# A spectral filter beside a feed-forward product: two kinds of step change places in each slot, and one small copy changes its engine

## The chip, the cores and the metric

The kernel runs on one core of one Trainium2 chip. The core has TensorE (PE, matrix products into PSUM), VectorE (DVE), ScalarE (ACT), GpSimd (POOL) and SyncE (SP); SP, ACT and POOL also issue DMAs. Each engine works through its own list of instructions in order and waits on semaphores for the others. The metric is the time of one execution on the device, in microseconds (us).

## The reference

The input `x` has 2048 rows and 1024 columns. The layer norm of it goes two ways: through a filter in the frequency domain, and through a feed-forward product with a hidden width of 3584.

```
xn  = layernorm(x)
s   = irfft2(rfft2(xn) * (w_r + 1j * w_i), (2048, 1024))
h   = silu(xn @ w1)            # 2048 x 3584
out = x + s * silu(h @ w2)     # 2048 x 1024
```

## The kernel before

TensorE works in float16 and gets near float32 by splitting each operand into a high and a low half and adding three products: high by high, high by low, low by high. A split has two instructions: `high` on ScalarE (L257, the value rounded to f16) and `low` on VectorE (L260, the rest).

The feed-forward product comes in two parts. The **first product** fills the first 635 us: w1 by the rows of `xn`, in 112 pieces `pa` of 24 matmuls. The hidden values are combined and written to device memory as the left sides of a Strassen-like scheme with seven products. The **second product** fills the rest: for each of the seven products `m` (0 to 6) and each of eight row blocks `j` there is a PSUM tile `pb{m}_{j}`, made of two half-products (`k` = 0, 1) of 21 matmuls of 128x512 (L549 to L551). Each half-product needs its hidden values, `ht{m}_{j}_{k}`, loaded by a DMA that ACT issues (L525), and its half of w2, `w2_{m}_{k}`. Finished tiles are added by VectorE and ScalarE into `kept` and `pl` tiles, stored, and at the end combined with the filter's result (`fs`, `fx`) into the output.

w2 is made ready while the second product runs. There are 98 blocks `jr0` to `jr97`, 14 to each product. A step of `w2_gen` loads the block four ahead by a DMA on SP (L420), for products 4 and 5 adds a second block into the one three ahead by an accumulating DMA on POOL (L424; it waits for the first load to land), and then issues the high of its own block and the low of the block before it.

The filter has a forward transform, the multiplication by w, edge terms (`edge`, whose result comes back through memory as the tile `zps`) and an inverse transform. The inverse treats four groups of columns `c` in the order `IORDER = (1, 3, 0, 2)`. For each, `load_i` (L1234) loads its spectrum into the one tile `zt{c}` and the constants `kk{c}`, `edge_in` (L1246) copies the edge column into the tile, and `i_gen` (L1255) then makes, in steps: four matmul groups `iu{c}_{g}` (L1281 or L1289) in two PSUM buffers; for each, a copy `uc` of half of it by ScalarE (L1295), sum and difference `ub` by VectorE (L1297, L1298), which free the PSUM buffer, a butterfly (`up`, `uu`) on VectorE, and a split into `us` (L1360, L1361); then, when all four `us` are there, four matmul groups `id{c}_{p}` (L1371), which read the constants `cis`, with butterflies `sk`, `spa` and `s` on VectorE. The name `tag="ft"` is that of the two PSUM buffers that `iu` and `id` share.

The order of all instructions is set while the program is built, by Python generators. After each half-product of the second product the program calls `work()`, one **slot**. A slot gives one step to the queue `wq` (w2's steps), one to `xq`, and up to three to `bg` (transform, filter, inverse), until a step answers `PAUSE` or until the planner's own clock of VectorE is past its clock of TensorE by more than `LEAD`, 1.0 us. So what stands first in a slot stands first on every engine and in every DMA queue that its step uses. `while ready2[0] < ...` ahead of a half-product draws further w2 steps if the half of w2 that it needs isn't made yet.

The DMAs that SP and ACT issue share eight semaphores in turn; a DMA is issued when the one before it on its semaphore has landed.

Of the kernel before, what the change touches and what calls it, by code (L numbers as in the profile page):

```python
# [26 lines left out]
IORDER = (1, 3, 0, 2)  # L27
# [105 lines left out]
def spectral_ffn(ctx, tc, x, w_r, w_i, w1, w2, ca, kc, ci, tw, pm, out):  # L133
    nc = tc.nc
# [35 lines left out]
    zps = cp.tile([128, 2, 4, 4, 2], F16, name="zps")  # L170
# [284 lines left out]
    done2, ready2, chunks = [0], [-1], [0]  # L455
# [790 lines left out]
    def edge_in(c):  # L1246
        zt = C["z"][c]
        if c % 2:
            zt = zt.rearrange("m (e q h l i) -> m e q h l i", e=2, q=4, h=2, l=8)
            nc.gpsimd.tensor_copy(zt[:, :, :, :, 0, 0], zps[:, :, c])  # L1250
        else:
            zt = zt.rearrange("m (q h r l i) -> m q h r l i", q=4, h=2, r=2, l=8)
            nc.gpsimd.tensor_copy(zt[:, :, :, :, 0, 0], zp[:, c].rearrange("m r q h -> m q h r"))

    def i_gen(c):  # L1255
        ip = C["p"]
        tt, stt = nc.vector.tensor_tensor, nc.vector.scalar_tensor_tensor
        if c == IORDER[0]:
            edge_in(c)
# [187 lines left out]
        for p in range(5):  # L1447
            if p < 4:
                mat2(p)
            if p:  # L1450
                bfly(p - 1)
            if p == 3 and c != IORDER[-1]:
                edge_in(IORDER[IORDER.index(c) + 1])
            yield 3.4 if p else 0.3
# [13 lines left out]
    def slot(q):  # L1468
        while q:
            job = q[0]  # L1470
            cost = job.step()
            if not job.done:
                return cost
            if q and q[0] is job:
                q.pop(0)
        return 0
# [19 lines left out]
    with tc.manual_schedule():  # L1496
        bg, wq, xq = [], [], []
# [20 lines left out]
        def after(ev):  # L1518
            settle()
            fresh_ev[0] = ev  # L1520
            tick()
            work()

        def work():
            slot(wq)
            count[0] += 1
            if count[0] % 8:
                slot(xq)
            clock["dve"] = max(clock["dve"], clock["pe"] - 1.0)
            for _ in range(3):  # L1530
                if clock["dve"] > clock["pe"] + LEAD or hold[0] or slot(bg) == PAUSE:
                    break

        nc.gpsimd.memset(ones, 1.0)
        idle = ones.bitcast(F16)
# [105 lines left out]
        for n, (m, j) in enumerate(seq):  # L1641
# [14 lines left out]
            for k in range(2):  # L1656
                while ready2[0] < m * NP + 7 * k + 6:
                    slot(wq)
                mm2(m, j, ps, k)
                if k == 0:  # L1660
                    settle()
                    load_parts(m, j)
                    ahead_rows(m, j)
                    if (m, j) == (6, 6):
                        load_parts(m, 7)
                        ahead_rows(m, 7)
                    tick()
                    work()
# [43 lines left out]
```

## Time and profile before

| | us |
|---|---|
| three runs | 1228.38, 1229.09, 1229.4 |
| profiled execution: time | 1229.27 |
| profiled execution: span | 1227.5 |
| TensorE busy | 1211.4 (99%) |
| VectorE busy | 1003.7 (82%) |
| ScalarE busy | 496.1 (40%) |
| GpSimd busy | 140.2 (11%) |

The span goes from the first to the last instruction; the profiled execution's time is 1.8 us more. The granted TensorE clock is 1.000 over the span. Numbers of the profile are on the span's own clock. A row of a chain or a timeline begins with the start and the length in microseconds; a bracket at its end gives the engine's idle time ahead of it and what ended that. The profile leaves out the numbers in tile names: `zt` there is `zt1` or another, `jr` any block of w2; which one a row is follows from its place in the program's order.

### The profile page before, as it was taken

What the parts mean: (1) busy time and instruction counts of PE and PEld (TensorE: products, weight loads), DVE (VectorE), ACT (ScalarE), POOL (GpSimd) and SP (SyncE); (2) the same over time, 40 slices, a digit from 0 to 9 for tenths busy, and PEclk for the clock granted to TensorE, in tenths of its full rate; (3) what the DMA queues carried; (4) which work ended last, traced back from release to release, by engine and by line L of the source; (5) the groups of instructions that cost most, each with busy time, mean ns of one, the idle gap of its engine ahead of it and who ended that gap; (6) DMA issues with size and microseconds to landing.
All of it is one profiled execution on the core that took longest, in us unless ns stands there. A gap on an engine that the chain in (4) does not pass through costs nothing.

```text
span 1227.5 us, 19143 instructions
## 1 busy us (share of the span) xinstructions
PE 1211.4 (99%) x6992; PEld 615.1 (50%) x6992; DVE 1003.7 (82%) x2006; ACT 496.1 (40%) x670; POOL 140.2 (11%) x256
## 2 busy tenths in 40 slices
PE   8999999999999999999999999999999999999998
PEld 5544445445444544445445555554445554455545
DVE  7778997898798798958969989995377876997766
ACT  6775553455375654434423222221122322333212
POOL 3320100002010000201101121152111111000000
PEclk9999999999999999999999999999999999999999
DMA  8887585747678978489998999977979999996677
GB/s 251 184 195 188 165 255 180 211 130 214 192 254 276 317 231 270 146 259 208 188 282 279 263 253 233 315 255 221 269 218 302 264 338 310 305 364 244 224 249 274
DMA packets 285055, 299.98 MB, mean 244 GB/s; under 512 B 48928, under 2 KB 211744, under 8 KB 284576
## 3 DMA queue, kind: packets, MB, share of 16 engines
q1 hardware_dynamic: 264944, 239.95, 66.9%
q10 hardware_dynamic: 15840, 50.67, 11.8%
q0 software_dynamic: 4176, 8.13, 3.6%
q8 instruction: 55, 0.90, 0.3%
q14 instruction: 40, 0.33, 0.1%
HBM read 188.05 MB, written 104.35 MB: 238 GB/s over the span
## 4 chain that ended last, share of the span: by engine, by line
PE 59%; DMA 15%; DVE 14%; ACT 3%; issue 3%; SPq 1%; POOL 1%; ACTq 0%; DVEq 0%; POOLq 0%
PE pa L466 33%; PE pb L551 7%; PE pb L549 7%; PE pb L550 7%; DMA jr<-in_B_w_dram 2%; PE id L1371 2%; DMA jr<-ws 1%; DVE Z L1124 1%; DVE w L260 1%; DMA cis<-in_ci_dram 1%; DMA ht<-hd_dif 1%; ACT xp L750 1%; DMA vq<-vd 1%; DMA zd<-zq 1%; DMA zt<-zd 1%
## 5 line engine op out<-in xcount | busy, mean ns | idle before, releaser
L466 PE MATMUL pa<-xnT,w 128*128 128x512 f16 x2688 | 584.3, 379 | 1.3 <-ACT w L257 0.7
L466 PEld LDWEIGHTS <-w 128*128 128x128 f16 x2688 | 261.2, 98 | 312.7 <-issue 1.2
L549 PE MATMUL pb<-w,ht 128*128 128x512 f16 (+2 forms) x812 | 300.4, 372 | 0.0
L550 PE MATMUL pb<-w,ht 128*128 128x512 f16 (+2 forms) x812 | 300.4, 372 | 0.0
L551 PE MATMUL pb<-w,ht 128*128 128x512 f16 (+2 forms) x812 | 300.3, 372 | 0.0
L551 PEld LDWEIGHTS <-ht 128*128 128x128 f16 x812 | 79.4, 98 | 91.1
L549 PEld LDWEIGHTS <-ht 128*128 128x128 f16 x812 | 79.5, 98 | 86.7
L550 PEld LDWEIGHTS <-ht 128*128 128x128 f16 x812 | 79.4, 98 | 86.8
L475 ACT ACTIVATE h<-pa,s 128x512 f32<-128x512 f32 x112 | 75.6, 677 | 77.6 <-PE pa L466 60.2
L257 ACT ACTIVATE w<-jr,sc 128x512 f16<-128x512 f32 x98 | 68.4, 713 | 86.4 <-DMA jr<-in_B_w_dram 45.6
L260 DVE SCALAR_TENSOR_TENSOR w<-jr,sc,w 128x512 f16<-128x512 f32 x98 | 71.3, 743 | 18.8 <-ACT w L257 18.8
L257 ACT ACTIVATE hosum<-hr,hs 128x1536 f16<-128x1536 f32 x28 | 44.0, 1573 | 87.5 <-DVE hr L505 34.9
L260 DVE SCALAR_TENSOR_TENSOR hoone<-h,hs,hoone 128x2048 f16<-128x2048 f32 x28 | 65.6, 2342 | 7.2 <-ACT hoone L257 7.2
L257 ACT ACTIVATE hoone<-h,hs 128x2048 f16<-128x2048 f32 x28 | 55.9, 1995 | 28.6 <-issue 11.1
L504 DVE TENSOR_TENSOR hr<-h 128x1024 f32<-128x1024 f32 x28 | 34.1, 1219 | 21.8 <-ACT h L475 21.8
L260 DVE SCALAR_TENSOR_TENSOR hosum<-hr,hs,hosum 128x1536 f16<-128x1536 f32 x28 | 50.7, 1810 | 1.4 <-ACT hosum L257 1.4
L257 ACT ACTIVATE w<-w1r,rs 128x1024 f16<-128x1024 f32 x28 | 31.9, 1143 | 37.7 <-DVE w L260 24.2
L642 ACT ACTIVATE pl<-pl,c 128x512 f32<-128x512 f32 (+2 forms) x28 | 17.7, 656 | 70.2 <-DVE pl L618 43.6
L424 POOL DMA_DIRECT2D jr<-in_B_w_dram x28 | 24.6, 999 | 180.3 <-DMA jr<-in_B_w_dram 89.7
L1124 POOL TENSOR_TENSOR Z<-yb 128x32 f32<-128x32 f32 x32 | 16.2, 525 | 209.0 <-DVE yb L1103 202.2
L1033 ACT ACTIVATE zq<-Z,zs 128x1024 f16<-128x1024 f32 x16 | 18.4, 1148 | 52.5 <-DVE Z L1124 25.6
L260 DVE SCALAR_TENSOR_TENSOR w<-w1r,rs,w 128x1024 f16<-128x1024 f32 x28 | 35.6, 1273 | 2.3 <-ACT w L257 2.2
(239 smaller groups left out, 1571.6 us busy)
## 6 DMA issues: line engine op xcount, KB each, us to landing
w1r<-in_B_w_dram SPq DMA_DIRECT2D x28, 512.0 KB, 6.6
hd_sum<-hosum SPq DMA_DIRECT2D x56, 256.0 KB, 2.9
hd_one<-hoone SPq DMA_DIRECT2D x56, 256.0 KB, 4.0
hd_dif<-hoone SPq DMA_DIRECT2D x56, 256.0 KB, 4.3
w2m<-in_B_w_dram SPq DMA_DIRECT2D x28, 512.0 KB, 5.6
ht<-hd_dif ACTq DMA_DIRECT2D x32, 448.0 KB, 9.2
jr<-in_B_w_dram SPq DMA_DIRECT2D x56, 256.0 KB, 6.7
ht<-hd_sum ACTq DMA_DIRECT2D x32, 448.0 KB, 5.7
```

Source lines behind the costliest of these rows:

```text
L257: nc.scalar.activation(hi, raw, AF.Copy, scale=scale)
L260: nc.vector.scalar_tensor_tensor(lo, raw, scale, hi, op0=OP.mult, op1=OP.subtract)
L424: nc.gpsimd.dma_start(raw[n], w2_block(*todo[n], 1), accum_op=OP.add)
L466: nc.tensor.matmul(ps, w[:, wh, d], xt[:, xh, d], start=(n == 0), stop=(n == 23))
L475: nc.scalar.activation(hq[:, 2 * (c % 2) + f % 2], ps, AF.Silu, scale=s1[:, f:f + 1])
L504: tt(sums[:, 0:2], hq[:, 0::2], hq[:, 1::2], op=OP.subtract)
L549: nc.tensor.matmul(ps, hh[:, 0], w[:, 0], start=first, stop=False)
L550: nc.tensor.matmul(ps, hh[:, 0], w[:, 1], start=False, stop=False)
L551: nc.tensor.matmul(ps, hh[:, 1], w[:, 0], start=False, stop=last)
L1033: nc.scalar.activation(zqs[q][:, 0, :, 16 * j:16 * j + 16], zs_[u], AF.Copy, scale=zs)
L1124: eng.tensor_tensor(Z[:, ns, pos], x0[:, :, ls], x1[:, :, ls], op=o_)
L1371: nc.tensor.matmul(ps[:, g, cols], us[g][:, uh, 4 * r + p], C["ci"][:, ch, g, r, cols], start=(r == 0 and n == 0), stop=(r == 1 and n == 2 ...
```

## The change

In the second product (`chunks[0] == 4`) a slot's step of w2 comes after the steps of `bg`. In the first product it stays ahead. And the copy of the edge column for the first group of the inverse, `c = 1`, is made by VectorE; those of the other three groups stay on GpSimd. The computation is the same, and so are the instructions but for that one.

```diff
@@ edge_in
         if c % 2:
             zt = zt.rearrange("m (e q h l i) -> m e q h l i", e=2, q=4, h=2, l=8)
-            nc.gpsimd.tensor_copy(zt[:, :, :, :, 0, 0], zps[:, :, c])
+            (nc.vector if c == IORDER[0] else nc.gpsimd).tensor_copy(zt[:, :, :, :, 0, 0], zps[:, :, c])
@@ work
         def work():
-            slot(wq)
+            if chunks[0] < 4:
+                slot(wq)
             count[0] += 1
             if count[0] % 8:
                 slot(xq)
             clock["dve"] = max(clock["dve"], clock["pe"] - 1.0)
             for _ in range(3):
                 if clock["dve"] > clock["pe"] + LEAD or hold[0] or slot(bg) == PAUSE:
                     break
+            if chunks[0] == 4:
+                slot(wq)
```

In the lists below, a row is the line, the kind of instruction, the tile written and the tiles read; the last number in a name counts buffers.

SP's list where the inverse is opened, in the last slots of product 2; before:

```order
L420 DMA jr53_8542<-in_B_w2_dram 128x512
L1215 DMA zps_220<-zpd_87 64x4x8 x4
L420 DMA jr54_8572<-in_B_w2_dram 128x512
L1239 DMA zt1_8581<-zd1_84 64x8x512 x4
L1243 DMA kk1_8586<-in_kc_dram 128x2064
L1229 DMA cis_8580<-in_ci_dram 128x4096
L420 DMA jr55_8619<-in_B_w2_dram 128x512
```

The same place after:

```order
L420 DMA jr53_8542<-in_B_w2_dram 128x512
L1215 DMA zps_220<-zpd_87 64x4x8 x4
L1239 DMA zt1_8577<-zd1_84 64x8x512 x4
L1243 DMA kk1_8582<-in_kc_dram 128x2064
L1229 DMA cis_8576<-in_ci_dram 128x4096
L420 DMA jr54_8588<-in_B_w2_dram 128x512
L420 DMA jr55_8619<-in_B_w2_dram 128x512
```

The load of `jr54` has moved behind `zt1`, `kk1` and `cis`. On POOL the copy into `zt1` stood there, before:

```order
L424 DMA jr56_8644<-in_B_w2_dram 128x512
L424 DMA jr57_8675<-in_B_w2_dram 128x512
L424 DMA jr58_8701<-in_B_w2_dram 128x512
L1250 COPY zt1_8581<-zps_220 128x16
L424 DMA jr59_8733<-in_B_w2_dram 128x512
```

It now stands on DVE, between the lows of `jr54` and `jr55`, after:

```order
L598 TENSOR_TENSOR kept5_7103<-kept5_7103,pb2_5_8652 128x512
L260 SCALAR_TENSOR_TENSOR w2_3_1_8544<-jr54_8588,sc2_234,w2_3_1_8544 128x512
L1250 COPY zt1_8577<-zps_220 128x16
L260 SCALAR_TENSOR_TENSOR w2_3_1_8544<-jr55_8619,sc2_234,w2_3_1_8544 128x512
L598 TENSOR_TENSOR kept6_7180<-kept6_7180,pb2_6_8710 128x512
```

In this place DVE otherwise has the same rows as before, and ACT has the high of `jr54`, the loads of `ht3_0_0` and `ht3_0_1`, and the high of `jr55` in this order in both programs.

ACT's list in product 4, where group `c = 0` of the inverse begins (`uc0_0` is the copy that starts to empty the PSUM of `iu0_0`); before:

```order
L525 DMA ht4_7_0_10426<-hd_one_3_1_97 128x1792
L525 DMA ht4_7_1_10428<-hd_one_3_1_97 128x1792
L257 ACTIVATE w2_5_1_10302<-jr81_10299,sc2_234 128x512
L1295 ACTIVATE uc0_0_10520<-iu0_0_10470 128x512
L1341 ACTIVATE up0_0_10526<-ub0_0_10522 128x8
L1342 ACTIVATE up0_0_10526<-ub0_0_10522 128x8
L642 ACTIVATE pl4_4_1_10383<-pl4_4_1_10383,c2_233 128x512
L257 ACTIVATE w2_5_1_10302<-jr82_10327,sc2_234 128x512
L1360 ACTIVATE us0_0_10588<-uu0_0_10525 128x1024
```

The same place after:

```order
L525 DMA ht4_7_0_10426<-hd_one_3_1_97 128x1792
L525 DMA ht4_7_1_10428<-hd_one_3_1_97 128x1792
L1295 ACTIVATE uc0_0_10516<-iu0_0_10466 128x512
L1341 ACTIVATE up0_0_10522<-ub0_0_10518 128x8
L1342 ACTIVATE up0_0_10522<-ub0_0_10518 128x8
L257 ACTIVATE w2_5_1_10302<-jr81_10299,sc2_234 128x512
L642 ACTIVATE pl4_4_1_10383<-pl4_4_1_10383,c2_233 128x512
L1360 ACTIVATE us0_0_10584<-uu0_0_10521 128x1024
L1295 ACTIVATE uc0_1_10587<-iu0_1_10491 128x512
```

`uc0_0` and the two small copies of `up0_0` have moved ahead of the high of `jr81`, and the high of `jr82` has left the rows shown: it now stands behind the two small copies of `up0_1`.

TensorE's list where the first half of `pb3_0` ends; before:

```order
L550 LDWEIGHTS ht3_0_0_8706
L550 MATMUL pb3_0_8938<-w2_3_0_8188,ht3_0_0_8706 128x512
L551 LDWEIGHTS ht3_0_0_8706
L551 MATMUL pb3_0_8938<-w2_3_0_8188,ht3_0_0_8706 128x512
L549 LDWEIGHTS ht3_0_1_8708
L549 MATMUL pb3_0_8938<-w2_3_1_8544,ht3_0_1_8708 128x512
```

The same place after:

```order
L550 LDWEIGHTS ht3_0_0_8706
L550 MATMUL pb3_0_8938<-w2_3_0_8203,ht3_0_0_8706 128x512
L551 LDWEIGHTS ht3_0_0_8706
L551 MATMUL pb3_0_8938<-w2_3_0_8203,ht3_0_0_8706 128x512
L1281 LDWEIGHTS zt1_8577
L1281 MATMUL iu1_3_8961<-kk1_8582,zt1_8577 128x128
```

The group `iu1_3` now follows the first half of `pb3_0` and not the second. In the same way `id1_0` to `id1_3` come one half-product earlier, and `iu3_0` to `iu3_3` and `id3_0` to `id3_2` one or two. From `id3_3` on TensorE's order is the same as before. In product 3, `zt3` and `kk3` are likewise loaded ahead of `jr66`, and the copy into `zt3` stands on POOL ahead of the accumulating DMA of `jr67`.

## The prediction

> **What bounds the kernel now.** I read the page's shares first, then TensorE's waits, then the stretches of time around the two long ones, then the chain that leads into each, and last what the engines in that chain had been waiting for.
>
> ```profile
> PE 1211.4 (99%) x6992; PEld 615.1 (50%) x6992; DVE 1003.7 (82%) x2006; ACT 496.1 (40%) x670; POOL 140.2 (11%) x256
> PE iu L1281 <- POOL zt L1250: 2.6, 1, 2.6
> PE iu L1289 <- DVE ub L1298: 1.8, 1, 1.8
> 860.00:880.00 20.00, 17.39 (x85) 7.80 (x83) 2.70 (x4) 0.72 (x1) 3.33 (x6) 1.00 1.02 302
> 880.00:1020.00 140.00, 140.00 (x927) 75.64 (x924) 109.75 (x285) 40.82 (x75) 19.17 (x24) 1.00 0.96 278
> 1020.00:1040.00 20.00, 18.18 (x136) 10.19 (x134) 10.77 (x21) 3.73 (x8) 1.80 (x3) 1.00 0.95 312
> 1040.00:1220.00 180.00, 180.00 (x1113) 94.97 (x1110) 142.89 (x299) 51.04 (x96) 1.13 (x2) 1.00 0.81 285
> ```
>
> TensorE is the bound. In the stretches (start and end, length, then busy time of PE, PEld, DVE, ACT, POOL; granted clock, DMA share, GB/s) it is busy without a gap from 880 to 1020 and from 1040 to 1220, short of 2.61 us before 880 and of 1.82 us before 1040, which are the two waits above. VectorE is 78% busy (109.75 of 140), so it has room. The granted clock is 1.00 in each stretch. A change that only reorders this work can win those two holes and no more; it loses wherever it makes a new one.
>
> The chain into the first hole, then what TensorE, ACT, DVE, POOL and SP show there:
>
> ```profile
> 860.43 14.25 DMA cis<-in_ci_dram
> 874.75 2.60 DMA jr<-in_B_w_dram
> 877.35 0.61 POOL jr L424 x2
> 876.73 0.38 PE L551 MATMUL pb<-w,ht 128*128 128x512 f16 x1
> 879.72 0.95 PE L1281 MATMUL iu<-kk,zt 128*128 128x128 f16 x14 [2.61 <-POOL zt L1250]
> 854.48 4.86 ACTq L525 DMA_DIRECT2D ht<-hd_sum  x2
> 875.37 0.72 ACT L257 ACTIVATE w<-jr,sc 128x512 f16<-128x512 f32 x1 [21.93 <-DMA jr<-in_B_w_dram]
> 876.12 0.75 DVE L260 SCALAR_TENSOR_TENSOR w<-jr,sc,w 128x512 f16<-128x512 f32 x1 [11.22 <-ACT w L257]
> 878.41 1.26 POOL L1250 COPY zt<-zps 128x16 f16<-128x16 f16 x1
> 865.04 12.20 SPq L420 DMA_DIRECT2D jr<-in_B_w_dram  x7
> L1239 SPq DMA_DIRECT2D zt<-zd x4: 573/783/3536, 849.2 to 851.5; - x4
> DMA to landing us min/median/max: 11.2/16.4/19.6
> ```
>
> The last two rows are those of the four `zt1` loads, issued from 849.2 to 851.5, so the copy's data was there by 851.5 + 19.6 = 871.1. But the copy stands on POOL behind three accumulating DMAs of w2, and those wait for direct loads that SP issued behind `zt1`, `kk1` and `cis`. It ran at 878.4. Matmuls start every 0.22 us here, so from the start at 876.73 to the one at 879.72 PE lost 2.99 - 0.22 = 2.8 us.
>
> The chain into the second hole:
>
> ```profile
> 1026.42 9.80 DMA jr<-in_B_w_dram
> 1036.25 0.72 ACT L257 ACTIVATE w<-jr,sc 128x512 f16<-128x512 f32 x1 [11.88 <-DMA jr<-in_B_w_dram]
> 1036.87 0.59 ACT uc L1295
> 1029.57 2.91 PE L1289 MATMUL iu<-kk,zt 128*128 128x129 f16 x48
> 1036.64 0.38 PE L551 MATMUL pb<-w,ht 128*128 128x512 f16 x1
> 1038.83 0.34 PE L1289 MATMUL iu<-kk,zt 128*128 128x129 f16 x3 [1.81 <-DVE ub L1298]
> ```
>
> `iu0_0` and `iu0_1` were through by 1032.5, but ScalarE's copy `uc0_0`, which begins to empty their PSUM, stands on ACT behind the w2 step of `jr81`, and that waited 11.9 us for an accumulating DMA. So `ub0_0` came late and `iu0_2` with it: 1038.83 - 1036.64 - 0.22 = 2.0 us.
>
> **The change part by part.** *The copy on VectorE, and SP's order.* `zt1`, `kk1` and `cis` are now issued ahead of `jr54`'s load; the copy leaves POOL's queue and stands on DVE between the lows (L260) of `jr54` and `jr55`. Its new wait is therefore `jr54`: load, high on ACT, low, copy. The trace has no such copy on VectorE; the nearest row is
>
> ```profile
> L1209 DVE SCALAR_TENSOR_TENSOR zp<-edge,zs,zp x1: 251/251/251, 836.8 to 836.8; 128x32 f16<-128x32 f32 x1
> ```
>
> so 0.25 us (tiny f16 result, like the copy), against 1.26 us as on POOL. At the late end `jr54` lands where `jr55` did, the next load behind `cis`: high from 875.37, low from 876.12 to 876.87, copy to 877.1 (at POOL's price 878.1). TensorE comes to `iu1_0` at 876.73 + 0.22 = 876.95, so the hole is 0.2 us at most (1.2 at POOL's price) instead of 2.8. At the early end the two `ht3_0` loads, which ACT issued at 854 to 859 between these transfers, now stand behind `jr54`'s high and no longer share the DMA engines. From 849.2 to 874.7 SP's loads of `zt1` (128 x 8192 f16, 2 MB), `kk1` and `cis` moved, with the page's sizes
>
> ```profile
> kk<-in_kc_dram SPq DMA_DIRECT2D x1, 516.0 KB, 17.0
> cis<-in_ci_dram SPq DMA_DIRECT2D x1, 1024.0 KB, 14.2
> ht<-hd_sum ACTq DMA_DIRECT2D x4, 448.0 KB, 7.2
> ```
>
> 3.6 MB, and `ht3_0` 0.9 MB beside them: 4.5 MB or more in 25.5 us, 0.18 MB/us. Without the 0.9 MB `cis` lands up to 5 us earlier, and the copy ends at 872 to 874, with 3 us or more to spare. I take the middle, the hole gone: -2.8 us; ends -1.6 and -2.8. The Trainium skill ("DMA: Bandwidth & Descriptors", section "Issuing engines are not separate DMA queues") says that DMAs of the scalar and sync engines run on the same 16 engines and interleave. By that rule the early end holds; if the two queues had engines of their own, the late one would, 0.2 us worse. The DMA share of 1.02 in 860 to 880, with both queues at work, agrees with it.
>
> *What pays for it there.* `ht3_0` is issued at 872 to 876 instead of 854. `pb3_0` needs it after the second `iu` pair, `pb2_7_1` and `iu1_2`.
>
> ```profile
> 882.58 0.22 PE pb L549
> 887.11 1.34 PE iu L1281 x24
> DMA to landing us min/median/max: 4.3/8.1/9.8
> ```
>
> A half-product is 887.11 - 882.58 = 4.53, so the need is at 876.95 + 2 x 1.34 + 4.53 + 1.34 = 885.5. With the longest landing of the `ht` loads in this stretch, 9.8 us, one issued at 875.5 is there at 885.3; with the median 8.1, at 883.6. Cost 0, at worst about 1.
>
> *Reordered slots.* In product 3 `iu1_3`, `id1` and `iu3_0` to `iu3_3` come one or two half-products (4.5 us each) earlier on TensorE, because VectorE's clock in the planner is no longer past its limit when their step is asked. In-order TensorE would wait if their inputs do not come forward equally.
>
> ```profile
> 889.66 0.68 DVE L1298 TENSOR_TENSOR ub<-iu,uc 128x512 f32<-128x512 f32 x1
> 897.51 1.34 PE iu L1281 x24
> 911.51 1.22 DVE L1361 SCALAR_TENSOR_TENSOR us<-uu,us 128x1024 f16<-128x1024 f32 x1
> 921.51 3.05 PE id L1371 x48
> ```
>
> Taking 2.8 us and one half-product off: `iu1_3` is reached at 897.5 - 2.8 - 4.5 = 890.2, its PSUM is freed by `ub1_1` at 890.3 - 2.8 = 887.5: 2.7 us to spare. `id1_0` is reached at 921.5 - 7.3 = 914.2, `us1_3` ends at 912.7 - 2.8 = 909.9: 4.3 to spare. Cost 0, hidden by those margins; if VectorE came later than that, each us would be a us.
>
> *w2's steps go behind.* The same 98 highs and lows, each later by at most the steps of one slot. The least margin of a low before its first matmul is in product 5:
>
> ```profile
> 1050.76 1.41 DVE L260 SCALAR_TENSOR_TENSOR w<-jr,sc,w 128x512 f16<-128x512 f32 x2
> 1067.49 0.38 PE L549 MATMUL pb<-w,ht 128*128 128x512 f16 x1
> ```
>
> The second of these lows (`jr83`'s) ends at 1052.1; by the program's order its half is begun at 1067.5, 15 us on. A slot's inverse step is 2 to 6 us of VectorE. Cost 0.
>
> *`uc0_0` ahead of `jr81`.* ACT now does `uc0_0` when `iu0_0` is done (1029.57 + 1.4, less 2.8), 8 us or more before its old place; `iu0_2` no longer waits: -2.0 us. What is late next is the low of `us0_3`, which the last quarter of `id0_0` reads:
>
> ```profile
> 1071.55 1.22 DVE L1361 SCALAR_TENSOR_TENSOR us<-uu,us 128x1024 f16<-128x1024 f32 x1 [0.43 <-ACT us L1360]
> 1073.32 2.87 PE L1371 MATMUL id<-cis,us 128*128 128x130 f16 x42
> ```
>
> It ended at 1072.8, and with half of the 3.05 us of a pair of `id` groups (the fence before last) the quarter began at 1073.5 + 3/4 x 1.53 = 1074.6: 1.8 us to spare. TensorE now comes 4.8 us sooner, so `us0_3` has to be 3.0 us sooner. Its row of VectorE work starts 8 us sooner, but w2's lows in it still wait for their accumulating DMAs. If those land 2.8 us sooner with everything else, `us0_3` is 0.2 us late at most; if not at all, up to 1.5; both are estimates, added up from the durations of that row's steps. I take 0.2.
>
> *Sum*: -2.8 - 2.0 + 0.2 = -4.6 us against the profiled execution's own 1229.27 us (span 1227.5): 1224.7. The median of the runs, 1229.09, is 0.2 below that execution, so the time is 1224.5.
>
> **The rivals.** *One hole stays or comes back.* The copy is held by `jr54`, or `us0_3` is late by 1.5 and `ht3_0` by 1. For it: the copy still waits for a transfer behind `cis`. Against: 3 us of margin if the queues share. If only the second hole goes, 1229.1 - 2.0 = 1227.1; only the first, 1226.3.
>
> *The holes only move.* The same deliveries set the pace, and the inverse's steps stall further on: 1228.5 to 1229.5. For it: DMA shares of 0.91 to 1.02. Against: both holes come from waiting in a queue behind work that was not theirs, not from a late input.
>
> *Slower: `jr54` lands late.* The copy now has w2's delivery in front of it, and both `ht3_0` loads stand behind the same high. Every us that `jr54` lands after 875.2 is one of TensorE at `iu1_0` (0.72 + 0.75 + 0.25 from landing to copy's end, need at 876.95). To end 2.5 us above the time before, the new hole has to be 2.8 + 2.0 + 2.5 = 7.3 us, with `jr54` at 882.5: 1231.6. `ht3_0`, issued at 883 and there by 893 at the longest, adds nothing, since its need moves to 892.8 with the hole. For it: this stretch has transfers of up to 19.6 us. Against: fewer bytes are in front of `jr54` than were in front of `jr55`, which landed at 875.4.
>
> *The reordering does nothing* is excluded by the order of the queues.
>
> **How the numbers follow.** Both holes gone with up to 1 us given back: 0.64, 1223.6 to 1225.8. One of them: 0.17, 1226.0 to 1227.6. Only moved: 0.08. Slower: 0.11. The range 1223.6 to 1228.2 leaves out the last two. About 0.2%, 2.5 us, is what a measurement can tell from no change. Below 1226.6 lie the first case and a third of the second: faster 0.70; same 0.18; slower 0.12.
>
> **What would show it.** Right: no TensorE wait over 0.5 us on `zt` (L1250) or `ub` (L1298); the copy, as a DVE row of 0.2 to 0.3 us, ends between 872 and 877; `uc0_0` starts within 1 us of `iu0_0`'s end; TensorE busy 20.00 of 20 us in both stretches. Wrong: a TensorE wait on `ht` at `pb3_0`, on `us` at `id0_0`, or on `zt` with the copy behind a low that waits for a `jr`.

## The result

Over 22 executions each the median went from 1229.59 us to 1226.45 us. The ratio is 0.9974, with a 95% interval from 0.9964 to 0.9984: 2.0 to 4.4 us less. In two later sets, on two chips, the changed kernel's ratio was 0.9990 (0.9975 to 1.0006) and 0.9989 (0.9972 to 1.0005). So it is faster by 3.2 us in the first set and by 1.2 and 1.4 us in the two others, whose intervals just take in no change; by none of the three ratios is it the 4.6 us that the sum gave.

Single executions scatter over all sets between about 1224 and 1234 us (changed) and 1226 and 1237 us (before). Much of that goes with the mean granted clock, which is on record for each execution. Of the 46 executions of the changed kernel in its three sets, nine have a clock of 1.000 and take 1223.84 to 1226.55 us, and the 22 at 0.997 or below take 1227.91 to 1234.37 us. Of the 82 executions of the kernel before in the three sets that followed the first, twelve have 1.000 and take 1226.17 to 1229.29 us. The means of these two groups with the full clock, 1225.2 and 1228.0, differ by 2.8 us.

Both holes are gone. These are, of the changed kernel, the page's shares, the one row in TensorE's list of waits that lies behind 640 us, and the stretches that answer to those shown of before:

```profile
PE 1213.9 (99%) x6992; PEld 616.3 (50%) x6992; DVE 1004.1 (82%) x2007; ACT 494.7 (40%) x670; POOL 137.0 (11%) x255
PE eps L1161 <- POOL edge L1154: 1.1, 1, 1.1
860.00:880.00 20.00, 20.00 (x94) 9.06 (x93) 3.21 (x6) 1.44 (x2) 3.63 (x4) 1.00 1.05 316
880.00:1020.00 140.00, 140.00 (x928) 75.78 (x927) 111.83 (x291) 39.84 (x74) 18.67 (x23) 1.00 0.95 277
1020.00:1040.00 20.00, 20.00 (x147) 11.30 (x146) 10.89 (x21) 5.65 (x10) 1.75 (x2) 1.00 1.02 305
```

TensorE is busy 20.00 of 20 us in both stretches that had a hole. The engines at the first place, in the timeline of the changed kernel, and the copy `uc0_0` at the second:

```profile
873.77 0.72 ACT L257 ACTIVATE w<-jr,sc 128x512 f16<-128x512 f32 x1 [19.01 <-DMA jr<-in_B_w_dram]
874.53 0.75 DVE L260 SCALAR_TENSOR_TENSOR w<-jr,sc,w 128x512 f16<-128x512 f32 x1 [6.57 <-ACT w L257]
875.20 0.20 DVE L1250 COPY zt<-zps 128x16 f16<-128x16 f16 x1
880.66 2.84 PE L1281 MATMUL iu<-kk,zt 128*128 128x128 f16 x48
1032.13 0.60 ACT L1295 ACTIVATE uc<-iu 128x512 f32<-128x512 f32 x1 [4.08 <-DMA ht<-hd_one]
```

The copy waits for `jr54`, as it was read from the order; it takes 0.20 us on VectorE and is done at 875.40, with TensorE there at 880.66. `uc0_0` starts at 1032.13, about 0.2 us behind the matmuls of `iu0_0`, and no longer waits for the DMA of `jr81`.

TensorE came late to both places, though, and the reason is the one wait in the list that the kernel before does not have. It stands at the nine small matmuls of the edge step (`eps`, L1161 to L1163), between `pb1_7` and `pb2_0`. First the kernel before, then the changed one. Of the timeline: TensorE's last matmul of `pb1_7` and first edge matmul, GpSimd's first edge copy, and VectorE's row that leads there; and the stretch from 808 to 812, whose third number from the end is the granted clock.

```profile
804.63 0.38 PE L551 MATMUL pb<-w,ht 128*128 128x512 f16 x1
804.84 0.30 PE L1161 MATMUL eps<-edge,perm 128*128 128x24 f32 x2
804.18 0.37 POOL L1154 COPY edge<-xsv 128x24 f32<-128x24 f32 x1
796.61 1.28 DVE L1038 SCALAR_TENSOR_TENSOR zq<-Z,zs,zq 128x1024 f16<-128x1024 f32 x1 [2.45 <-ACT zq L1033]
798.94 1.22 DVE L1086 TENSOR_TENSOR T<-X,wq 128x1024 f32<-128x1024 f32 x1
800.19 0.69 DVE L1099 TENSOR_TENSOR T<-T,T 128x512 f32<-128x512 f32 x1
808.00:812.00 4.00, 4.00 (x27) 2.08 (x26) 4.00 (x8) 0.37 (x2) 0.00 (x0) 1.00 0.98 328
```

```profile
805.21 0.38 PE L551 MATMUL pb<-w,ht 128*128 128x512 f16 x1
806.66 0.40 PE L1161 MATMUL eps<-edge,perm 128*128 128x24 f32 x2 [1.07 <-POOL edge L1154]
806.24 0.37 POOL L1154 COPY edge<-xsv 128x24 f32<-128x24 f32 x1
798.14 1.29 DVE L1038 SCALAR_TENSOR_TENSOR zq<-Z,zs,zq 128x1024 f16<-128x1024 f32 x1 [4.22 <-ACT zq L1033]
800.48 1.22 DVE L1086 TENSOR_TENSOR T<-X,wq 128x1024 f32<-128x1024 f32 x1
801.62 0.74 DVE L260 SCALAR_TENSOR_TENSOR w<-jr,sc,w 128x512 f16<-128x512 f32 x1
802.28 0.68 DVE L1099 TENSOR_TENSOR T<-T,T 128x512 f32<-128x512 f32 x1
808.00:812.00 4.00, 4.00 (x18) 2.10 (x18) 3.90 (x10) 1.52 (x3) 0.48 (x4) 0.61 1.02 214
809.47 0.63 PE L550 MATMUL pb<-w,ht 128*128 128x512 f16 x1
809.90 0.63 PE L551 MATMUL pb<-w,ht 128*128 128x512 f16 x1
```

Two things are to be seen. A low of w2 (`jr41`'s, L260 at 801.62) now stands in the middle of the filter's steps, and from the low of `zq` to the edge copy it takes 806.24 - 798.14 = 8.10 us instead of 7.57. Beside that, ScalarE's `zq` ahead of it came later. And after the wait of 1.2 us the granted clock is 0.61 in the next 4 us: 512-column matmuls start every 0.43 us instead of 0.22. The trace's record of the clock has it at half for 3.41 us, from 808.90 on. TensorE loses the wait of 1.2 us, some 1.7 us to the clock, and 0.2 us at the edge matmuls themselves, which take longer here.

The whole second product can be put in one table. All 6992 matmuls stand in each trace (7004 in `fill` below, which has twelve more), so the time between the first matmuls of named half-products can be taken from their starts. The stretches are: *edge*, from the start of `pb1_7`'s second half to the start of `pb2_1`; *zt1*, from there to `pb4_0`; *uc0*, from there to `pb5_0`; *rest*, to the last matmul. From `pb0_0` to the edge stretch it is 165.18 us in every execution. The first line is the kernel before in us; the others are differences to it.

| kernel | edge | zt1 | uc0 | rest |
|---|---|---|---|---|
| before | 17.71 | 155.59 | 86.11 | 162.85 |
| changed | +3.14 | -2.79 | -1.99 | 0.00 |
| changed, second and third execution (runs below) | +3.83, +6.01 | -2.79, -2.79 | -1.99, -1.99 | 0.00, 0.00 |
| before, second execution (run below) | +0.54 | +1.58 | -0.30 | 0.00 |

The two gains are the predicted 2.8 and 2.0 us, and the same in each of the three executions of the changed kernel. What was not in the sum is the first column.

### The profile page after: what moved, and what is told of

Its sections match the earlier page's. It is cut to its first block, busy times and chain, and to the rows that moved or that the text cites. A ratio compares the mean times of both kernels' runs of the same rounds, so it can differ in the third digit from the quotient of the medians.

```text
span 1226.4 us, 19138 instructions
## 1 busy us (share of the span) xinstructions
PE 1213.9 (99%) x6992; PEld 616.3 (50%) x6992; DVE 1004.1 (82%) x2007; ACT 494.7 (40%) x670; POOL 137.0 (11%) x255
## 4 chain that ended last, share of the span: by engine, by line
PE 69%; DMA 10%; DVE 10%; ACT 3%; issue 2%; SPq 1%; POOL 0%; ACTq 0%; DVEq 0%; POOLq 0%
PE pa L466 33%; PE pb L549 10%; PE pb L550 10%; PE pb L551 10%; DMA zd<-zq 2%; PE id L1371 2%; DMA ht<-hd_dif 2%; DMA wq<-in_A_w_i_dram 1%; ACT xp L750 1%; DMA jr<-ws 1%; DMA jr<-in_B_w_dram 1%; PE iu L1289 1%; DMA ws<-wd 1%; PE iu L1281 1%; DVE wd L383 1%
## 5 line engine op out<-in xcount | busy, mean ns | idle before, releaser
L260 DVE SCALAR_TENSOR_TENSOR w<-jr,sc,w 128x512 f16<-128x512 f32 x98 | 71.9, 744 | 17.9 <-ACT w L257 17.8
L260 DVE SCALAR_TENSOR_TENSOR hoone<-h,hs,hoone 128x2048 f16<-128x2048 f32 x28 | 65.6, 2342 | 6.9 <-ACT hoone L257 6.9
L260 DVE SCALAR_TENSOR_TENSOR hosum<-hr,hs,hosum 128x1536 f16<-128x1536 f32 x28 | 50.7, 1811 | 1.4 <-ACT hosum L257 1.4
L260 DVE SCALAR_TENSOR_TENSOR w<-w1r,rs,w 128x1024 f16<-128x1024 f32 x28 | 35.6, 1273 | 2.3 <-ACT w L257 2.2
```

The costliest lines, as they stand in the source:

```text
L260: nc.vector.scalar_tensor_tensor(lo, raw, scale, hi, op0=OP.mult, op1=OP.subtract)
```

## The experiments

Theory: each hole is a fixed arrival less TensorE's own time; the change takes two arrivals out of w2's queue, and makes a third one, the edge copies, later. Rivals: the edge wait is an accident; or deliveries set the pace, so that a hole closed at one place opens at the next.

**The changed kernel again** (`after_again`, no edit).

> The changed kernel once more. My theory, three holes that add up: both old holes of TensorE are gone (no wait on zt before iu1_0, none on ub before iu0_2), and a new one stands at the edge matmuls (L1161 to L1163) near 806 us, because GpSimd's edge copies now come after one more low of w2 on VectorE: 1.2 us of waiting, and in executions where the clock is let down after it, some 1.6 us more of matmuls at half the clock. Ratio to the kernel before 0.9965 to 0.9985. Rival, the wait at the edge was an accident of one execution: no wait over 0.6 us there this time, and a ratio of 0.996 (-4.8 us).

Ratio 0.9990 (0.9975 to 1.0006), above the 0.9965 to 0.9985 that I expected. No wait on `zt` or `ub`; at the edge the wait was longer, and the clock fell again (TensorE's list of waits, and two stretches):

```profile
PE eps L1161 <- POOL edge L1154: 1.7, 1, 1.7
808.00:812.00 4.00, 3.90 (x23) 2.60 (x23) 3.90 (x9) 2.01 (x3) 1.39 (x9) 0.82 1.04 173
812.00:816.00 4.00, 4.00 (x16) 1.60 (x14) 4.00 (x6) 0.00 (x0) 0.00 (x0) 0.75 1.01 363
```

So it is not an accident of one execution.

**The new order only behind the edge** (`from_2_2`).

```diff
-            if chunks[0] < 4:
+            late = chunks[0] == 4 and place[0] >= 18   # place: 8 * product + row block
+            if not late:
                 slot(wq)
...
-            if chunks[0] == 4:
+            if late:
                 slot(wq)
```

> The step of w2 goes behind only from row block 2 of product 2 on, so that the stretch up to the edge matmuls has the order of before, and the rest that of the changed kernel. If the edge hole is caused by the new order: the wait at the edge matmuls is under 0.6 us, the clock is 1.00 from 804 to 816, both old holes stay gone, and the time is 4 to 5 us below the kernel before (ratio 0.9960 to 0.9968), 1.2 to 3.1 us below the changed kernel. If deliveries set the pace and holes only move: the copy into zt1 is late again now that TensorE comes 3.1 us earlier, a wait of 1 to 3 us before iu1_0, and the time is that of the changed kernel.

Ratio 0.9971 (0.9953 to 0.9990), 2.35 us below the changed kernel's median on the same chip. The two gains are there whole (-2.79, -1.99), so the holes do not move. But the edge was not quiet: a wait of 0.75 us between starts, the clock at 0.57 behind it, +2.66 us. This expectation failed, and the ratio is above the 0.9960 to 0.9968 that went with it. The way from `zq` to the edge copy was 7.57 us again, as in the old order; what came late was `zq` itself, which ScalarE starts when an earlier `zq` has been stored (timeline, list of waits, stretch):

```profile
796.15 1.15 ACT L1033 ACTIVATE zq<-Z,zs 128x1024 f16<-128x1024 f32 x1 [9.45 <-DMA zd<-zq]
PE eps L1161 <- POOL edge L1154: 0.6, 1, 0.6
808.00:812.00 4.00, 4.00 (x13) 1.43 (x11) 3.92 (x8) 0.78 (x3) 0.00 (x0) 0.57 1.01 320
```

In the first execution of the kernel before this row starts at 795.42. So the old order has the edge wait too, in part of its executions.

**Work for TensorE in the wait** (`fill`).

```diff
         ps = pf.tile([128, 512], F32, name="eps", tag="ff")
+        fill, now = ones.bitcast(F16), dict(clock)
+        for _ in range(12):
+            nc.tensor.matmul(ps[:, 256:512], fill[:, 0:128], fill, start=True, stop=True)
+        clock.update(now)
```

> The changed kernel with 12 matmuls of 128x256 on constants (1.3 us) ahead of the edge matmuls, into columns of their PSUM tile that nothing reads; all else in the same order. TensorE is kept at work through the wait. If the granted clock falls because of the wait, it now stays 1.00 from 806 to 816, and in the profile TensorE loses 1.3 to 1.8 us from the end of pb1_7 to the start of pb2_1 against the kernel before, not 3.1. If the clock falls for another reason (the small matmuls of the edge, whose columns are few): it still falls to about 0.5 for 3 us, and the loss is 3.1 or more.

Ratio 0.9986 (0.9969 to 1.0003). The wait was 1.31 us of filling and 0.89 us more, 2.2 us in all, longer than the 1.9 us of `after_again`; and the clock stayed up (timeline of TensorE, stretch):

```profile
804.76 1.47 PE L1162 MATMUL eps<-ones 128*128 128x256 f16 x12
806.96 0.40 PE L1165 MATMUL eps<-edge,perm 128*128 128x24 f32 x2 [0.73 <-POOL edge L1154]
808.00:812.00 4.00, 4.00 (x26) 2.57 (x26) 3.90 (x9) 1.81 (x3) 0.79 (x7) 1.00 0.97 215
```

The stretch lost 2.43 us, more than the 1.3 to 1.8 expected, since the wait itself was longer; it was under the 3.83 of `after_again`. In this execution, then, the clock did not fall behind a wait of which TensorE spent more than half at work, with the small matmuls as they were. It did fall in other executions behind idle waits shorter than the 0.89 us that were left, so one execution does not show that the filling kept it up.

**The copy alone on VectorE** (`copy_only`: the kernel before with the one line of `edge_in`).

> The kernel before, with the copy into zt1 on VectorE and the old order; it stands there behind the low of jr55. If GpSimd's queue of accumulating DMAs was what held the copy: it starts 0.1 us after that low, ends near 877.1, and the hole before iu1_0 shrinks from 2.8 us to 0.4 or less; the hole before iu0_2 stays at 2.0; 2.5 us below the kernel before (ratio 0.9975 to 0.9985). If the holes only move: 2 us or more of it comes back at a later wait of TensorE, and the ratio is 0.999 to 1.001.

Ratio 0.9990 (0.9972 to 1.0008), in the rival's range; but nothing came back at a later wait of TensorE, and the loss lies ahead, at the edge. There was no wait before `iu1_0` (-2.79), and uc0 kept its hole. The copy ended at 878.4, 1.3 us later than expected. And the edge wait of 0.64 us with the clock's fall made TensorE 2.53 us later there, and that closed the hole as much as the copy did (timeline):

```profile
878.23 0.20 DVE L1250 COPY zt<-zps 128x16 f16<-128x16 f16 x1
879.16 2.84 PE L1281 MATMUL iu<-kk,zt 128*128 128x128 f16 x48
```

Without the 2.53 us TensorE would have been there at 876.6, and the copy, behind the low of `jr55`, at 878.4: 1.8 us would have been left by this reckoning.

**The order alone** (`order_only`: the changed kernel with that copy on GpSimd).

> The changed order with the copy into zt1 on GpSimd again, behind the accumulating DMAs of jr56 to jr58. In the changed kernel's trace these were issued up to 878.4, so the copy would be done at about 879.5, and TensorE, late by the edge wait, came to iu1_0 at 880.7. Theory: the moved loads alone bring the copy forward by 1 us only, but the edge wait covers the rest: a wait of 0 to 1 us before iu1_0, and the time is that of the changed kernel within 1.5 us. Rival, the engine of the copy is what counts: the wait before iu1_0 is 2 to 3 us as in the kernel before, and the time is 2 us or more above the changed kernel.

Ratio 0.9994 (0.9980 to 1.0007). No wait before `iu1_0` either, as the theory had it, and again because TensorE was late (edge +2.51; timeline):

```profile
877.47 1.15 POOL L1250 COPY zt<-zps 128x16 f16<-128x16 f16 x1
879.05 2.84 PE L1281 MATMUL iu<-kk,zt 128*128 128x128 f16 x48
```

On a TensorE that is on time, at 876.5, this copy would be 2.1 us late. The engine alone and the order alone bring the copy to 878.4 and 878.6; both together to between 874.8 and 877.4 in the eight executions that had both.

**The new order only up to the edge** (`until_2_2`: the comparison turned round, and the copy on GpSimd).

> The new order only up to row block 2 of product 2, the old from there on, and the copy on GpSimd: what the first stretch costs by itself. Edge wait of 1.2 to 2.2 us, with the clock at half behind it in most executions: TensorE 3 us later at pb2_1 than in the kernel before. The hole before iu1_0 then shrinks from 2.8 to under 0.8 us, as the copy's end at 879.7 doesn't depend on TensorE (theory: a hole is a fixed arrival less TensorE's own time); if that hole stays at 2 us or more, its arrival moves along with TensorE. The hole before iu0_2 stays at 1.5 to 2.0. Time from 1 us below to 3 us above the kernel before.

Ratio 1.0005 (0.9990 to 1.0021). The edge wait was 0.11 us, below all that I had expected for the new order: ScalarE's `zq` started at 795.47 this time. The hole before `iu1_0` was 1.8 us instead of 2.8, with TensorE 0.6 us later in the span than in the kernel before and the copy's end 0.4 us earlier. That fits an arrival of its own, but TensorE moved too little for a proof.

**The kernel before again** (`before_again`, no edit, one execution).

> The kernel before, another execution. The holes before iu1_0 (2.8 us) and iu0_2 (2.0 us) are there again within 0.6 us, the wait at the edge matmuls is 0 to 0.8 us. If a hole can let the clock down, as in the five executions looked at behind the edge matmuls, rows of matmuls at twice their distance may stand behind one of the two holes this time; if these two cannot, none do.

The holes were 2.7 and 1.7 us, the edge wait 0.3. And here the clock fell behind the first hole; the 48 matmuls of `iu1_0` and `iu1_1` took 4.30 us, in the first execution of this kernel 2.85 (timeline, and two stretches):

```profile
879.64 4.30 PE L1281 MATMUL iu<-kk,zt 128*128 128x128 f16 x48 [2.55 <-POOL zt L1250]
880.00:882.00 2.00, 2.00 (x29) 2.00 (x27) 0.00 (x0) 0.58 (x1) 1.22 (x2) 0.70 0.93 199
882.00:884.00 2.00, 2.00 (x20) 1.89 (x18) 1.95 (x5) 0.14 (x2) 0.00 (x0) 0.50 1.11 210
```

So a hole of the same length costs 2.8 us in one execution and 4.4 in another (155.59 and 157.16 us for the stretch zt1, which takes 152.80 us without a hole). This is part of the scatter between executions.

**The edge matmuls one half-product later** (`late_eps`, and again as `late_eps_2`: the changed kernel with one step of `edge_gen` drawn behind the end of a step of the filter instead of ahead of it; on TensorE the nine matmuls move behind the first half of `pb2_0`, and nothing else moves on any engine).

```diff
-            if u > 13:
-                next(B["edge"])
             yield 2.3
+            if u > 13:
+                next(B["edge"])
```

> The changed kernel with the nine edge matmuls one half-product later on TensorE, behind the first half of pb2_0; nothing else moves on any engine. So far the wait before them was 1.2 and 1.9 us in the changed kernel, and the clock fell to half for 3 us behind it both times. If that wait and the clock behind it are what was given back: no wait over 0.3 us there, clock 1.00 from 804 to 820, no other new wait, and a time 3 us below the changed kernel, 4 to 6 us below the kernel before (ratio 0.995 to 0.9968). If the clock falls on account of the small matmuls themselves: it falls here too, and 1.6 us of the 3 stay lost. If the holes only move: the copy into zt1 comes too late for the earlier TensorE, 1 us or more before iu1_0.

Ratio 0.9954 (0.9935 to 0.9974), and executions from 1224.51 to 1226.36 us. No wait at the edge and no fall of the clock there, so the small matmuls with nothing ahead of them to wait for did not let it down. A wait that the edge had covered came up instead, for `ht2_0` (list of waits, stretch, and the timeline at `iu1_0`):

```profile
PE pb L549 <- DMA ht<-hd_dif: 0.5, 1, 0.5
808.00:812.00 4.00, 4.00 (x32) 3.03 (x31) 3.90 (x9) 1.76 (x2) 1.03 (x8) 1.00 0.98 226
877.00 0.20 DVE L1250 COPY zt<-zps 128x16 f16<-128x16 f16 x1
877.41 2.84 PE L1281 MATMUL iu<-kk,zt 128*128 128x128 f16 x48
```

The copy into `zt1` is now only just in time: 0.12 us lost before `iu1_0`. The differences to the kernel before are edge +0.46, zt1 -2.67, uc0 -1.99.

Last, four kernels were timed on one chip:

> The changed kernel a third time, beside the three below on the same chip. From the rows so far: 8.1 us from VectorE's low of zq to GpSimd's first edge copy (7.6 in the old order), an edge wait of 0.6 to 2.2 us, and the clock at half for 3 us behind it if the wait is 0.6 us or more. Ratio 0.997 to 0.999. If the clock's fall has nothing to do with the length of the wait, it is absent behind a long one this time, or present behind one under 0.3 us.

> The changed kernel with the edge matmuls one half-product later, a second time. Theory: no wait and no fall of the clock at the edge matmuls, a wait of 0 to 0.8 us for ht2_0 ahead of pb2_0; ratio 0.9945 to 0.9970 and 2 to 5 us below the changed kernel on this chip. Rival, the first result was luck of the chip: the medians of the two are within 1 us.

> The kernel before with the edge matmuls one half-product later and nothing else. If the edge wait with the clock's fall behind it also cost the kernel before something in part of its executions (0, 0.3, 0.6 and 0.75 us in four executions with the old order, the clock down in two): 1 to 2 us below the kernel before (ratio 0.9982 to 0.9995), both old holes present. If it cost the kernel before nothing: 0.9995 to 1.0005. Then late_eps owes all of its gain to the two old holes and to the new order's own wait.

> The new order from row block 2 of product 2 on, with the edge matmuls one half-product later. If the new order of the first stretch makes ht2_0 and the edge copies late by more than the 0.54 us of the low that stands in the row: ScalarE's zq starts near 795.8 as in the old order's other executions (it was 795.3 to 797.9 in the new order's), no wait for ht2_0, and a time within 1 us of late_eps_2 or below it. If that start is only scattered by the DMAs: it lies anywhere from 795.3 to 797.9, and the time is that of late_eps_2 within 1 us. Both: copy into zt1 in time, no hole over 0.5 us in product 3 to 6.

| kernel | ratio to before | interval | edge | zt1 | uc0 | rest |
|---|---|---|---|---|---|---|
| changed (`after_third`) | 0.9989 | 0.9972 to 1.0005 | +6.01 | -2.79 | -1.99 | 0.00 |
| changed, edge later (`late_eps_2`) | 0.9958 | 0.9943 to 0.9972 | -0.18 | -2.79 | -1.99 | 0.00 |
| before, edge later (`late_before`) | 1.0012 | 0.9997 to 1.0026 | -0.18 | +0.07 | -0.35 | 0.00 |
| `from_2_2`, edge later (`late_from_2_2`) | 0.9952 | 0.9940 to 0.9964 | -0.18 | -2.79 | -1.99 | +0.66 |

In `after_third` the wait was 2.45 us and the clock stayed at half for about 7 us, twice as long as in the first trace (timeline, stretches):

```profile
806.55 0.40 PE L1161 MATMUL eps<-edge,perm 128*128 128x24 f32 x2 [2.29 <-POOL edge L1154]
808.00:812.00 4.00, 4.00 (x16) 2.58 (x16) 3.90 (x9) 1.51 (x3) 0.37 (x3) 0.50 0.97 251
812.00:816.00 4.00, 4.00 (x14) 1.51 (x12) 4.00 (x5) 0.00 (x0) 0.00 (x0) 0.65 1.01 398
```

The expectation for `after_third` had the wait at 2.2 us at most and the fall at 3 us; both were longer.

With the edge matmuls out of the way the change is worth 0.42 and 0.48% here, 5.2 and 5.9 us of 1231.1, and the sum's 4.6 us lie in both intervals. Their medians are also 5.5 and 6.1 us below the changed kernel's on this chip; the two do not differ beyond their intervals. Of the 13 executions of `late_eps` and `late_eps_2` twelve have a mean clock of 0.999 or 1.000, against 14 of the 46 of the changed kernel. In the trace of `late_eps_2` TensorE is on time and the copy is there before it (timeline):

```profile
875.26 0.20 DVE L1250 COPY zt<-zps 128x16 f16<-128x16 f16 x1
877.37 2.84 PE L1281 MATMUL iu<-kk,zt 128*128 128x128 f16 x48
```

`late_before` missed the 1 to 2 us that I expected: the same move gives the kernel before nothing. Its holes show why: TensorE waited until 879.86 for the copy there, until 879.72, 879.64 and 879.33 in the other three executions with the old copy. What it saves at the edge it waits for at `iu1_0`. Only in the changed kernel, where nothing behind the edge takes up the time, is each us lost at the edge a us of the end.

In `late_from_2_2` `zq` started at 794.60, earlier than in all others, and there was no wait for `ht2_0`; in `late_eps_2`, with the new order, it started at 795.78 and there was none either. Over all traces this start lies from 794.6 to 796.2 in the six with the old order up to the edge, and from 795.3 to 797.9 in the eight with the new. That the new order itself delays it is likely by these numbers, and not shown.

The start of `zq` does decide the wait, though, once it is taken from TensorE's own start of the second product (`pb0_0`). In the kernel before it comes 160.29 us behind that start, in the three executions of the changed kernel 161.25, 161.92 and 162.47. In each trace with the edge matmuls in their old place, the wait is what this distance has over 160.54 us in the old order and over 160.00 in the new, to within 0.03 us. So the moved low accounts for 0.54 us of each wait, and the waits of 1.2, 1.9 and 2.5 us would still have been 0.7, 1.4 and 1.9 us without it. The rest is the late start of `zq`, whose cause stays open.

## Why the prediction was right in part

The time, 1226.45, lies in the range, and the direction was right. The forecast was 4.6 us and the measured gain 2.0 to 4.4. Both gains of the sum were right in mechanism and size. That the time fell into the range all the same is in part luck: a loss that no term names took back a third of the gains or more, and the range had room for it only because it allowed for an old hole that stays.

- *The copy on VectorE, and SP's order*, -2.8 us: right, -2.79 in each execution. 0.25 us for the copy was 0.20. `jr54`'s high came at 873.8 in the first trace, 1.6 us ahead of `jr55`'s in the kernel before and not 3 or more; the early end of the estimate was too early, and where TensorE was on time, the copy had 1.9 us in hand in `late_eps_2` (done at 875.5 for 877.4), and none in `late_eps`.
- *`uc0_0` ahead of `jr81`*, -2.0 us: right, -1.99.
- *`us0_3` late next*, +0.2, at most 1.5: not there in the changed kernel, whose TensorE was late. In `late_from_2_2` it came up, 0.66 us, and in `late_eps` and `late_eps_2` it did not. The row of TensorE's timeline in `late_from_2_2`:

```profile
1070.57 0.68 PE L1371 MATMUL id<-cis,us 128*128 128x130 f16 x8 [0.49 <-DVE us L1361]
```

- *What pays for it there*, `ht3_0`, and *reordered slots* in product 3: right, no wait at any of them.
- *w2's steps go behind*, "Cost 0": this step failed. I looked at how much margin w2's own results have, and not at what the moved lows now stand in front of. Ahead of the edge copies, a low that stood in front of two steps of the filter now stands between them, 0.54 us in the way, in a place where TensorE had no time in hand: in the kernel before the first copy was done 0.28 us ahead of the matmul that needs it. The row could have been read: GpSimd's edge copy from 804.18 to 804.55 and the edge matmul at 804.84 stood there. The low alone would have made a wait of some 0.3 us in that execution; the 0.7 to 1.9 us beyond its share in the three traces come from the late `zq`, which I had not looked at either.
- *The granted clock is 1.00 in each stretch*: true of the one execution, and I took a hole's price from it as the hole's length. A hole can cost 1.7 us more (3.41 us at half the clock), and the new one cost at least that beyond its wait in each of the three traces of the changed kernel: +3.1, +3.8 and +6.0 us where the wait was 1.2, 1.9 and 2.5. It is not so in every execution: nine of the 46 had a mean clock of 1.000. By their times these were 2.8 us below their like of the kernel before and not 4.8; what took the difference there, no trace shows.
- The rival *one hole stays or comes back* gave 1226.3 to 1227.1, near the time measured, but by another mechanism: neither old hole stayed. *The holes only move* fell with the second and third columns of the table, and *slower: `jr54` lands late* with the copy done by 877.4 in all executions of the changed order on VectorE.

## What to carry to other kernels

When steps change places in a shared slot, look for what the moved step now stands in front of, on every engine and at every place of the stretch, and not only for how late the moved step may be. A wait of the bounding engine is an arrival less its own time: time lost ahead of it can be free, and becomes dear when the wait is taken away. After closing holes, read the profile again for the places that had only tenths of a microsecond in hand; here moving nine small matmuls by one half-product brought 5.5 us where both kernels ran on one chip, more than the change alone, and nothing in the kernel before.

## What the hardware showed that was not expected

The granted clock fell to half behind short holes. At the edge matmuls, nine matmuls of 8 or 24 columns that take 2.1 us, it fell behind waits of 0.60, 0.64, 0.75, 1.23, 1.91 and 2.45 us, and not behind 0, 0.11 and 0.31 us, nor behind the 0.89 us that were left in `fill`. Behind the hole before `iu1_0` it fell in one execution (2.7 us) and not in three others (2.8, 2.8, 1.8); behind that before `iu0_2`, 1.4 to 2.0 us in five executions, it did not fall. It stayed down for 3.41 us in six of these seven falls, and for 6.83 us in `after_third`.

The Trainium skill ("TensorE: Matmul & The Clock Gate", section "Part 1: The HAM clock gate (the "warmup" mystery)") has the clock go to half after an idle window of about 3.4 us, which runs freely and does not start with the work. The length of the falls agrees with it, and a free-running window would explain that one hole costs now 2.8 us and now 4.4. That a whole idle window is needed does not agree: a wait of 0.60 us with the small matmuls behind it, 2.9 us in all (`order_only`), was enough. Whether the window's phase decides was not tried.
